# Seven block products instead of eight in the second layer's projection of a retention and feed-forward kernel

## The chip, the cores and the metric

One core of a Trainium2 chip runs the whole program. TensorE (PE) multiplies matrices, VectorE (DVE) and ScalarE (ACT) work on tiles element by element, GpSimd (POOL) does a little in the first stage, and SyncE (SP) issues nearly all transfers between DRAM and the chip's SBUF; products land in PSUM, eight banks of 128 x 512 floats, from which DVE and ACT read. The metric is the device time of one execution in microseconds, less is better.

## The reference, cut to what matters

```python
# q, k, v: (4, 8, 576, 64); seq 576, 8 heads
scores = matmul(q, k.T) / sqrt(64)
ret = scores * where(rel >= 0, gamma[h] ** rel, 0)      # rel = i - j
x = matmul(ret, v)                     # laid out as 2304 tokens x 512
# layer 1: w_gate, w_val (512 x 1536), w_out (1536 x 512)
g = x @ w_gate;  y = (g * sigmoid(g) * (x @ w_val)) @ w_out
# layer 2: w_in (512 x 2048), w_out (2048 x 512)
r = maximum(y @ w_in, 0);  out = (r * r) @ w_out        # 2304 x 512, float32
```

The weights arrive as 64-bit floating-point words (the inputs to the program are float64 for the weights) and have to be turned into float32 on the chip.

## The kernel before

**Three passes.** Each float32 operand is split into a high half that TensorE multiplies at one column a cycle (type fp32r) and a low half, the difference. `three` multiplies hi x hi, hi x lo and lo x hi into one PSUM bank, so each product of a 128 x 128 weight block with a slice of tokens is three matmuls. ACT makes the high half (`act.copy`), DVE the low half (a subtraction).

**Stages.** First the retention, 16 pairs of head pair and batch; its result is the tile `xy`, 4 slices of 128 features x 2304 tokens. Then layer 1 and layer 2, both over five chunks of tokens, four of 512 columns and chunk 2 of 256 (`CHUNKS`). In each chunk they go over the hidden blocks f of 128 (12 in layer 1, 16 in layer 2): the projection (`project`: 4 slices x 3 matmuls into bank `g` or `v`; layer 1 has two of these), the hidden values on ACT and DVE (`hidden1`: sigmoid and two products; `hidden2`: relu and square), their halves (`halves`, tiles `h_hi`, `h_lo`), and the output product of the hidden block before (`out1`, `out2`) into four banks `a0` to `a3` that add up over all f. Layer 1's output goes back into `xy`; layer 2's goes out to DRAM at the end of each chunk.

**Order.** In the layers the framework's scheduler sets the order on each engine: it lays the code's instructions out on a timeline of its own, so that rows can stand earlier or later than in the code. Layer 1 takes chunk 1 first, then the second half of chunk 0 (its first half was done during the retention and lies in DRAM as `part`), then 2, 3, 4. At a chunk's last hidden block the four slices of the next chunk's tokens are split (`split_x`, tiles `xh`, `xl`).

**Weights.** `prefetch` loads a unit (one weight block of 128 x 512, 512 KB of 64-bit words) on SP's queue into a `raw` tile or into a part of `xy` that lies idle; `conversion` is a generator that turns one unit into float32 `w` with three DVE operations on words, an addition (shown as ISA) and two ACT casts, and then into halves. `pump` advances it by one step between the other work: 4 steps a place in layer 1, 1 in layer 2. Layer 2's 32 units are converted in layer 1's last chunk and in layer 2's first chunk. Weights of layer 2 stay in SBUF as halves.

Of the kernel before, what the change touches and what calls it, by code (L numbers as in the profile page):

```python
# [9 lines left out]
F32 = mybir.dt.float32  # L10
# [17 lines left out]
CHUNKS = {  # L28
    1: [(0, 512), (512, 512), (1024, 256), (1280, 512), (1792, 512)],
    2: [(0, 512), (512, 512), (1280, 512), (1792, 512), (1024, 256)],  # L30
}
NCH = len(CHUNKS[1])
G0 = S // 2
# [12 lines left out]
PUMPS = {0: 1, 1: 4, 2: 1}  # L46
# [9 lines left out]
def retention_moe_kernel(  # L56
# [19 lines left out]
    raw_p = pool(ctx, "raw_p", 2)  # L76
    cv_p = pool(ctx, "cv_p", 1)
    xs_p = pool(ctx, "xs_p", 4)
    h_p = pool(ctx, "h_p", 2)
    t_p = pool(ctx, "t_p", 2)  # L80
    wa_p = pool(ctx, "wa_p", WA)
# [37 lines left out]
    order += [(2, what, f) for f in range(F2) for what in "io"]  # L119
# [4 lines left out]
    def prefetch(upto):  # L124

        while loads["next"] <= min(upto, len(order) - 1):
            i = loads["next"]
            if loads["pool"] < 2:
                loads["pool"] += 1
                raw_flat[i] = raw_p.tile([P, 1024], U32, tag="raw", name="raw")  # L130
                raw, back = raw_flat[i].rearrange("p (a n) -> p a n", a=2), None
            elif spare:
                back = spare.pop(0)
                raw = back.bitcast(U32)
            else:
                return
            loads["next"] += 1
            ph, what, f = order[i]
            src = (w1, w2)[ph - 1][f, :, ("gvo", "io")[ph - 1].index(what), :].bitcast(U32)
            sp.dma_start(out=raw, in_=src.rearrange("p (a n) -> p a n", a=2))  # L140
            raw_t[i] = raw, back
# [3 lines left out]
    homes = [in_a[u] for u in order[:3 * F1]] + [in_a[1, what, f] for f in range(F1) for what in "gvo"]  # L145
    homes = iter(homes)

    def weight_tiles(early=None):
        wp = wa_p if early or next(homes) else wb_p
# [10 lines left out]

    def conversion():
        ts = dve.tensor_scalar
        for i in range(len(order)):
            prefetch(max(i, min(i + 3, loads["cap"])))
            raw, back = raw_t[i]
            words = raw.rearrange("p a (n two) -> p a n two", two=2)
            low, high = words[:, :, :, 0], words[:, :, :, 1]
            low16 = raw.bitcast(U16).rearrange("p a (n four) -> p a n four", four=4)[:, :, :, 1]
            wt = cv_p.tile([P, 512], U32, tag="w", name="w", bufs=2)
            w_t[i] = wt  # L170
            w = wt.rearrange("p (a n) -> p a n", a=2)
            wf = w.bitcast(F32)
            act.activation(out=low, in_=low16, func=AF.Copy, scale=2.0**-13)
            act.activation(out=wf, in_=high.bitcast(F32), func=AF.Abs)
            yield
            ts(out=wf, in0=wf, scalar1=TINY, scalar2=HUGE, op0=ALU.max, op1=ALU.min)
            yield
            if i:
                parts_unit(i - 1)
            ts(out=w, in0=w, scalar1=3, scalar2=0x3FFFFFFF, op0=ALU.logical_shift_left, op1=ALU.bitwise_and)  # L180
            yield
            dve.scalar_tensor_tensor(
                out=w, in0=high, scalar=0xC0000000, in1=w, op0=ALU.bitwise_and, op1=ALU.bitwise_or
            )
            yield
            if back is None:
                adds = [(wt, raw_flat.pop(i).rearrange("p (n two) -> p n two", two=2)[:, :, 0])]
            else:
                adds = [(w[:, a], low[:, a]) for a in range(2)]
            for to, lo in adds:  # L190
                dve.tensor_tensor(out=to, in0=to, in1=lo, op=ALU.add)
# [7 lines left out]
        yield  # L199

    pumped = {"n": 0, "limit": 0}
    convert = conversion()

# [21 lines left out]
    xs, xs_w = {}, []  # L225

    def split_x(ph, n, cc):
        t0, m = CHUNKS[ph][n]
        src = xy[:, cc, t0:t0 + m]
        if ph == 2 and n == 0:  # L230
            xs_w.append(weight_tiles())
        if ph == 2 and n % 2 == 0:
            hi, lo = cut(xs_w[cc], 0, m)
        else:
            hi = xs_p.tile([P, N], F32R, tag="xh", name="xh")[:, :m]
            lo = xs_p.tile([P, N], F32R, tag="xl", name="xl")[:, :m]
# [13 lines left out]
    def project(ph, n, f, *cols, then=None):  # L250
# [3 lines left out]
        last = f == (F1, F2)[ph - 1] - 1  # L254
# [5 lines left out]
        if then is not None:  # L260
            for cc in range(CC):
                split_x(1, then, cc)
        elif 3 <= f < 3 + CC and (ph, n) != (2, NCH - 1) and (ph == 2 or n == NCH - 1):
            split_x(2, (n + 1) % NCH, f - 3)
# [41 lines left out]
    def hidden2(n, f):  # L306
        (ps,) = project(2, n, f, ("i", ("g", "v")[f % 2]))
        yield
        t = t_p.tile([P, 512], F32, tag="t", name="t")[:, :CHUNKS[2][n][1]]
        act.activation(out=t, in_=ps, func=AF.Relu)  # L310
        yield
        dve.scalar_tensor_tensor(
            out=t, in0=ps, scalar=0.0, in1=t, op0=ALU.max, op1=ALU.mult
        )
        yield
        halves((2, n, f), t)

    acc = {}
# [4 lines left out]
    def out1(n, f):  # L323

        f0, f1 = ((f // HALF) * HALF, (f // HALF + 1) * HALF - 1) if n == 0 else (0, F1 - 1)
# [10 lines left out]
        if n:  # L336
            assert all(back is None for _, back in raw_t.values())
# [14 lines left out]

    def out2(n, f):
        if f == 0:
            acc[2, n] = accs(CHUNKS[2][n][1] // P)
        h = hs.pop((2, n, f))
        ensure((2, "o", f))
        w = units[2, "o", f]
        for tt in range(CHUNKS[2][n][1] // P):
            three(acc[2, n][tt], cut(h, tt * P, P), w, f == 0, f == F2 - 1)  # L360
        if f == F2 - 1:
            for tt, a in enumerate(acc.pop((2, n))):
                if tt % 2 == 0:
                    o = raw_p.tile([P, 1024], U32, tag="raw", name="o_sb").bitcast(F32)
                t = o[:, (tt % 2) * 512:][:, :512]
                if tt % 2:
                    dve.tensor_copy(t, a)
                else:
                    act.copy(t, a)
                r0 = CHUNKS[2][n][0] + tt * P  # L370
                sp.dma_start(out=out[r0:r0 + P, :], in_=t)

# [190 lines left out]
    wb_p = pool(ctx, "wb_p", 3 * F1 - WA)  # L563
# [3 lines left out]

    segments = [(1, 1, 0, F1), (1, 0, HALF, F1)] + [(1, n, 0, F1) for n in range(2, NCH)]
    steps = [(ph, n, f, f == b - 1) for ph, n, a, b in segments for f in range(a, b)]
    follows = {s[1]: t[1] for s, t in zip(segments, segments[1:])}  # L570
    steps += [(2, n, f, False) for n in range(NCH) for f in range(F2)]

    def allowed(ph, n, f):
        if ph == 1 and n < NCH - 1:
            return 3 * F1
        return 3 * F1 + max(0, min(2 * (f - 1), 3 * (f - 1) - CC)) if ph == 1 else len(order)

    todo = [(1, 0, f) for f in range(HALF)]
    for ph, n, f, end in steps:
        pumped["limit"] = 5 * allowed(ph, n, f) + 7  # L580
        if f == 1 and (ph, n) in ((1, 1), (1, NCH - 1), (2, 0)):
            t0, m = CHUNKS[ph][n]
            loads["open"] = True
            loads["cap"] = (3 * F1 if n == 1 else len(order)) - 1
            spare.extend(xy[:, c:c + 2, t0:t0 + m] for c in (0, 2))
        if f == (F1, F2)[ph - 1] - 4:
            loads["open"] = False
            spare.clear()
        if (ph, n, f) == (1, 0, HALF + 1):
            sp.dma_start(out=xy[:, :, CHUNKS[1][0][0]:][:, :, :CHUNKS[1][0][1]], in_=part)  # L590
        step = hidden1(n, f, follows.get(n) if end else None) if ph == 1 else hidden2(n, f)
        for _ in step:
            pump(PUMPS[ph])
        for x in todo:
            (out1 if x[0] == 1 else out2)(*x[1:])
            if len(todo) > 1:
                pump(PUMPS[1])
        todo = [(ph, n, f)]
    out2(*todo[0][1:])
# [61 lines left out]
```

## Time and profile before

| what | value |
|---|---|
| time, median of 3 runs | 934.52 us (933.61 to 934.84) |
| span of the profiled execution | 934.4 us |
| PE busy, matmuls | 921.1 us (99%), 5146 |
| weight loads of PE (beside the matmuls) | 768.8 us (82%) |
| DVE busy | 465.9 us (50%), 850 instructions |
| ACT busy | 339.5 us (36%), 628 instructions |
| moved by DMA | 63.01 MB, 67 GB/s on average |

The profile is that of one execution; its span is the time from the first instruction to the last, and nothing lies around it that the table of runs would add (934.4 beside 934.52). Busy times are sums over all stages, so 50% for DVE is an average of stages in which it is nearly full and stages in which it is nearly idle. All instructions carry line 106, the helper through which the kernel records every operation, so groups are told apart by the names of tiles.

### The profile page before, as it was taken

The page shows a single profiled execution, that of the slowest core. Times are in us where ns is not written, and L with a number is a line of the kernel's source. Part 1 is how long each engine was busy: PE and PEld are TensorE (multiplying, and loading weights), DVE is VectorE, ACT ScalarE, POOL GpSimd, SP SyncE. Part 2 cuts the span into 40 slices and gives each one's busy share as a digit, 9 for nine tenths or more (in the row PEclk, how much of TensorE's full clock was granted, in tenths as well). Part 3 has the DMA queues.
Part 4 walks back from the last instruction along what each step waited for, and adds up shares of the span by engine and source line. Part 5 has one row for each costly group of instructions (what it writes and reads, how often), then busy time and mean ns, then how long its engine had stood idle before and what let it go on. Part 6 is the DMA issues. An engine that isn't in the chain of part 4 may idle for free.

```text
span 934.4 us, 12527 instructions
## 1 busy us (share of the span) xinstructions
PE 921.1 (99%) x5146; PEld 768.8 (82%) x5146; DVE 465.9 (50%) x850; ACT 339.5 (36%) x628; POOL 20.6 (2%) x39
## 2 busy tenths in 40 slices
PE   8899999999999999999999999999999999999998
PEld 6677788788889998888888888888888888888896
DVE  4678778797424242224898886242224223322332
ACT  3555455464212131113565564232223223222222
POOL 2111100000000000000000000000000000000000
PEclk9899999999999999999999999999999999999999
DMA  9767344442100000001334230010001000100000
GB/s 328 254 226 247 113 136 121 150 135 90 46 1 1 1 1 1 0 1 46 110 117 150 99 113 1 1 45 1 1 1 46 0 1 1 46 1 0 19 28 22
DMA packets 22168, 63.01 MB, mean 67 GB/s; under 512 B 2272, under 2 KB 3808, under 8 KB 22112
## 3 DMA queue, kind: packets, MB, share of 16 engines
q1 hardware_dynamic: 22112, 62.22, 19.7%
q8 instruction: 40, 0.66, 0.3%
q14 instruction: 16, 0.13, 0.1%
HBM read 56.44 MB, written 5.77 MB: 67 GB/s over the span
## 4 chain that ended last, share of the span: by engine, by line
PE 87%; DMA 6%; DVE 4%; ACT 2%; issue 1%; SPq 0%; ACTq 0%
PE a L106 33%; PE g L106 24%; PE v L106 24%; PE o L106 3%; PE s L106 2%; DMA raw<-in_w 2%; DVE w L106 2%; DMA xy<-in_w 2%; DMA kv_sb<-in_kv 1%; PE kvs L106 1%; DVE t L106 1%; DMA part<-part_sb 0%; DVE w_lo L106 0%; SPq L106 0%; ACT w L106 0%
## 5 line engine op out<-in xcount | busy, mean ns | idle before, releaser
L106 ACT ACTIVATE t<-g 128x512 f32<-128x512 f32 (+1 forms) x100 | 55.4, 554 | 208.5 <-PE g L106 208.3
L106 ACT CAST h_hi<-t 128x512 fp32r<-128x512 f32 (+1 forms) x134 | 77.1, 576 | 118.6 <-DVE t L106 112.9
L106 DVE TENSOR_TENSOR h_lo<-t,h_hi 128x512 fp32r<-128x512 f32 (+1 forms) x134 | 85.2, 636 | 68.6 <-ACT h_hi L106 68.1
L106 PE MATMUL g<-xh,w_hi 128*128 128x512 f32 (+1 forms) x304 | 113.9, 375 | 0.0
L106 PE MATMUL v<-xh,w_hi 128*128 128x512 f32 (+1 forms) x304 | 113.8, 375 | 0.0
L106 PE MATMUL g<-xl,w_hi 128*128 128x512 f32 (+1 forms) x304 | 113.3, 373 | 0.1
L106 PE MATMUL g<-xh,w_lo 128*128 128x512 f32 (+1 forms) x304 | 113.3, 373 | 0.0
L106 PE MATMUL v<-xh,w_lo 128*128 128x512 f32 (+1 forms) x304 | 113.2, 373 | 0.0
L106 PE MATMUL v<-xl,w_hi 128*128 128x512 f32 (+1 forms) x304 | 113.2, 372 | 0.0
L106 PE MATMUL a<-w_lo,h_hi 128*128 128x512 f32 x288 | 112.3, 390 | 0.0
L106 PE MATMUL a<-w_hi,h_hi 128*128 128x512 f32 x288 | 112.2, 390 | 0.0
L106 PE MATMUL a<-w_hi,h_lo 128*128 128x512 f32 x288 | 109.8, 389 | 0.0
L106 DVE TENSOR_TENSOR t<-g,t 128x512 f32<-128x512 f32 (+1 forms) x60 | 38.2, 636 | 85.8 <-ACT t L106 85.5
L106 PE MATMUL a<-h_lo,w_hi 128*128 128x512 f32 (+1 forms) x216 | 79.3, 367 | 0.4 <-DVE h_lo L106 0.4
L106 PE MATMUL a<-h_hi,w_lo 128*128 128x512 f32 (+1 forms) x216 | 78.6, 366 | 0.0
L106 DVE SCALAR_TENSOR_TENSOR t<-g,t 128x512 f32<-128x512 f32 (+1 forms) x40 | 25.5, 638 | 105.2 <-ACT t L106 105.1
L106 PE MATMUL a<-h_hi,w_hi 128*128 128x512 f32 (+1 forms) x216 | 76.8, 366 | 0.7 <-ACT h_hi L106 0.7
L106 DVE SCALAR_TENSOR_TENSOR t<-v,t 128x512 f32<-128x512 f32 (+1 forms) x40 | 25.6, 639 | 92.3 <-ACT t L106 92.0
L106 DVE TENSOR_SCALAR w<-w 128x512 f32<-128x512 f32 (+1 forms) x136 | 57.3, 422 | 23.1 <-ACT w L106 21.8
L106 PEld LDWEIGHTS g<-xh,w_hi 128*128 128x128 f32 x304 | 57.3, 188 | 10.4 <-ACT raw L106 0.2
L106 PEld LDWEIGHTS g<-xl,w_hi 128*128 128x128 f32 x304 | 57.3, 188 | 10.3 <-DVE xl L106 0.5
L106 PEld LDWEIGHTS v<-xh,w_hi 128*128 128x128 f32 x304 | 57.3, 188 | 10.2
(82 smaller groups left out, 1474.2 us busy)
## 6 DMA issues: line engine op xcount, KB each, us to landing
raw<-in_w SPq DMA_DIRECT2D x51, 512.0 KB, 3.6
xy<-in_w SPq DMA_DIRECT2D x17, 512.0 KB, 3.7
qk_sb<-in_qk SPq DMA_DIRECT2D x15, 576.0 KB, 4.9
kv_sb<-in_kv SPq DMA_DIRECT2D x15, 576.0 KB, 3.9
out<-o_sb SPq DMA_DIRECT2D x18, 256.0 KB, 2.2
part<-part_sb SPq DMA_DIRECT2D x4, 256.0 KB, 2.8
xy<-part SPq DMA_DIRECT2D x1, 1024.0 KB, 5.2
mask_sb<-in_mask SPq DMA_DIRECT2D x4, 128.0 KB, 7.2
```

What stands on the lines that cost most here:

```text
L106: i = op(*args, **kw)
```

## The change

Layer 1's hidden blocks and products stay. Three things change.

**Seven products.** Layer 2's tokens are taken as 3 pairs of blocks of 384 columns (`M2`; block p and the block 1152 tokens behind it), its input features as two halves of 256, its hidden blocks as 8 pairs. For each pair of tokens and each pair of hidden blocks, a *system* n of 24, the four output blocks (2 hidden blocks x 2 token blocks) come from seven products of a combined weight block with a combined token block instead of eight plain ones. Each product is 2 slices x 3 passes = 6 matmuls of 384 columns. Products 1, 6, 7 and 4 add up in one bank (`g`) and are read off between (`x`), 5 and 3 in `v` (`y`), and 2 in `a0` (`z`); DVE adds the parts, squares and splits. The output product (`out_tile`) now takes 128 tokens and four hidden blocks at a time in banks `a1` to `a3` and adds to `xy`, which collects the sum over four groups and is stored at the last.

**Weight operands.** `conversion2` turns layer 2's words into float32 during layer 1 and stores them in DRAM (`wst`). The seven combined and split weight operands of a pair of hidden blocks (`stationary`, 11 DVE operations and 7 casts) are made in layer 1 for the first two pairs (`STAGED`) and in the first systems of layer 2 for the other six (`build`), and stored in DRAM (`win`). The systems of the later token pairs load them (`product`: 256 KB each), and output weights are loaded as float32 and split again for each group (`load_out`).

**Layer 1's order.** Chunks 1, 0, 3, 4 and then 2, the 256-wide one, last; there the hidden blocks 6 to 9 come first so that their weights' room (`freed`) can take the combined token blocks (`renew`, `operand`). Conversion is pumped at a pace (`PACE`, `SLOW`) per step. In chunk 2's end `stationary` operands of the tokens for the first pair are made.

```diff
-    2: [(0, 512), (512, 512), (1280, 512), (1792, 512), (1024, 256)],
+M2 = 384
+PAIRS2 = NT // (2 * M2)
+FP = F2 // 2
+PACE = {0: 1, 3: 1.5, 4: 1.5, 2: 0.8}
+SLOW = 1.25
+STAGED = 2
+FREED = range(6, 10)
+PORD = (1, 0, 2)
...
+    def stationary(k, w0, w1_, s1, to):
+        tt = dve.tensor_tensor
+        a11, a12, a21, a22 = (w[:, a:a + 256] for w in (w0, w1_) for a in (0, 256))
+        to(1, a11)
+        tt(out=s1, in0=a21, in1=a22, op=ALU.add)
+        to(2, a12)
+        to(5, s1)
+        tt(out=a21, in0=a11, in1=a21, op=ALU.subtract)
+        tt(out=a11, in0=s1, in1=a11, op=ALU.subtract)
+        to(6, a11)
+        to(7, a21)
+        tt(out=a12, in0=a12, in1=a11, op=ALU.subtract)
+        to(4, a22)
+        to(3, a12)
...
+            if j >= 2 * STAGED:
+                give_back(j)
+                late_store = wst[what, f], wf
+                continue
...
+            def to(i, src):
+                if len(stores) > 1:
+                    sp.dma_start(out=stores[-2][0], in_=stores[-2][1].bitcast(F32))
+                at = stage[len(stores) % 4]
+                split(at[:, :256], at[:, 256:], src)
+                stores.append((win[j // 2][:, ROW[i]], at))
...
+    segments = [(1, every), (0, every[HALF:]), (3, every), (4, every)]
+    segments.append((2, list(FREED) + [f for f in every if f not in FREED]))
...
+    wi_p = pool(ctx, "wi_p", 3)
...
+    def build(k):
+        w0, w1_ = (in_p.tile([P, 512], F32, tag=f"in{x}", name="w_in") for x in range(2))
+        for x, w in enumerate((w0, w1_)):
+            sp.dma_start(out=w, in_=wst["i", 2 * k + x])
...
+        def to(i, src):
+            w = wi_p.tile([P, 512], F32R, tag=f"wi{i}", name="wi")
+            split(w[:, :256], w[:, 256:], src)
+            built[k, i] = w
+            later.append((win[k][:, ROW[i]], w.bitcast(F32)))
...
+    def product(n, i, dst, first, last):
+        w = built.pop((n, i), None)
+        if w is None:
+            w = wi_p.tile([P, 512], F32R, tag=f"wi{i}", name="wi")
+            sp.dma_start(out=w.bitcast(F32), in_=win[n % FP][:, ROW[i]])
+        for c in range(2):
+            hi, lo = w[:, c * P:(c + 1) * P], w[:, 256 + c * P:256 + (c + 1) * P]
+            xh, xl = (x[:, c] for x in xo[i])
+            for k, (a, b) in enumerate(((hi, xh), (hi, xl), (lo, xh))):
+                at = c * 3 + k
+                pe.matmul(dst, a, b, start=first and at == 0, stop=at == 5, skip_group_check=True)
...
+    def slot(n, i):
...
+        if i == 1:
+            act.copy(a[:, 0], x)
+        elif i == 2:
+            tt(out=a[:, 0], in0=s["z"], in1=a[:, 0], op=ALU.add)
+            dve.scalar_tensor_tensor(out=a[:, 0], in0=a[:, 0], in1=a[:, 0], **relu2)
+        elif i == 6:
+            act.copy(b[:, 0], x)
+        elif i == 7:
+            act.copy(b[:, 1], x)
+            tt(out=b[:, 1], in0=s["y"], in1=b[:, 1], op=ALU.add)
+        elif i == 4:
+            act.activation(out=a[:, 1], in_=x, func=AF.Relu)
+            dve.scalar_tensor_tensor(out=a[:, 1], in0=x, in1=a[:, 1], **relu2)
+            hidden(n, "a", a)
+        elif i == 3:
+            tt(out=b[:, 0], in0=s["y"], in1=b[:, 0], op=ALU.add)
+            dve.scalar_tensor_tensor(out=b, in0=b, in1=b, **relu2)
+            hidden(n, "b", b)
...
+    def load_out(g):
+        for f in range(4 * (g % 4), 4 * (g % 4) + 4):
+            w = wo_p.tile([P, 2, 512], F32R, tag="wo", name="wo")
+            sp.dma_start(out=w[:, 1].bitcast(F32), in_=wst["o", f])
+            act.copy(w[:, 0], f32(w[:, 1]))
+            tt(out=w[:, 1], in0=f32(w[:, 1]), in1=f32(w[:, 0]), op=ALU.subtract)
...
+    def out_tile(g, which, j):
...
+        for k in range(4):
...
+            three(acc_, (hi, lo), (w[:, 0], w[:, 1]), k == 0, k == 3)
...
+        if q == 0:
+            act.copy(home, src)
+        else:
+            tt(out=home, in0=src, in1=home, op=ALU.add)
+        if q == 3:
+            sp.dma_start(out=out[t0:t0 + P, :].rearrange("p (c q) -> p c q", c=CC), in_=home)
...
+    for n in range(last + 2):
...
+        if n and n % 2 == 0:
+            load_out(n // 2 - 1)
+        for x in ((1, n), (7, n - 1), "o", (2, n), (4, n - 1), "o", (6, n), (3, n - 1), "o", (5, n)):
```

**Where the instructions stand.** At the end of layer 1's chunk 1, before the four splits of the next chunk's tokens, DVE has these rows before (`w` a weight unit, `t` and `h_lo` the hidden values and their low half, `xl` the low half of a slice of tokens; numbers tell tiles apart):

```order
L106 ISA w_2150<-raw_2148,w_2150 128x1024
L106 TENSOR_TENSOR t_2381<-g_2355,t_2381 128x512
L106 TENSOR_TENSOR t_2381<-v_2356,t_2381 128x512
L106 TENSOR_TENSOR h_lo_2386<-t_2381,h_hi_2385 128x512
L106 TENSOR_TENSOR xl_2428<-xy_81,xh_2427 128x512
L106 TENSOR_TENSOR xl_2432<-xy_81,xh_2431 128x512
L106 TENSOR_TENSOR xl_2436<-xy_81,xh_2435 128x512
L106 TENSOR_TENSOR t_2443<-g_2401,t_2443 128x512
L106 TENSOR_TENSOR xl_2440<-xy_81,xh_2439 128x512
L106 TENSOR_TENSOR t_2443<-v_2402,t_2443 128x512
L106 TENSOR_TENSOR h_lo_2448<-t_2443,h_hi_2447 128x512
```

And after, at the same place (`raw` now also holds the low halves of the staged operands, `s1` the sum that two of them share):

```order
L116 TENSOR_TENSOR t_2409<-g_2383,t_2409 128x512
L116 TENSOR_TENSOR s1_2728<-w_2675 128x256
L116 TENSOR_TENSOR w_2675<-w_2622,w_2675 128x256
L116 TENSOR_TENSOR raw_2620<-s1_2728,raw_2620 128x256
L116 TENSOR_TENSOR w_2622<-s1_2728,w_2622 128x256
L116 TENSOR_TENSOR t_2409<-v_2384,t_2409 128x512
L116 TENSOR_TENSOR raw_2618<-w_2675,raw_2618 128x256 x2
L116 TENSOR_TENSOR w_2622<-w_2622 128x256
L116 TENSOR_TENSOR raw_2620<-w_2622,raw_2620 128x256
L116 TENSOR_TENSOR h_lo_2414<-t_2409,h_hi_2413 128x512
L116 TENSOR_TENSOR raw_2620<-w_2622,raw_2620 128x256
L116 TENSOR_TENSOR xl_2456<-xy_81,xh_2455 128x512
```

The operations of the combined operands stand between the two products and the low half of the last hidden block but one, and ahead of the splits `xl`.

On SP, before, the only rows from layer 1's last chunk on are loads of `in_w2` into `raw` and `xy` and the stores of the output. After, these rows stand at the switch to layer 2 (`wi` weight operands of a product, `win` their place in DRAM, one for each pair of hidden blocks, `wst` float32 weights, `wo` output weights, `w_in` the weights that `build` combines):

```order
L116 DMA wi_4990<-win_83 128x512
L116 DMA w_in_4999<-wst_98 128x512
L116 DMA w_in_5000<-wst_100 128x512
L116 DMA wi_5003<-win_82 128x512
L116 DMA wi_5043<-win_82 128x512
L116 DMA wo_5103<-wst_91 128x512
L116 DMA wo_5107<-wst_93 128x512
L116 DMA wo_5111<-wst_95 128x512
L116 DMA wi_5023<-win_83 128x512
L116 DMA wo_5115<-wst_97 128x512
L116 DMA w_in_5129<-wst_102 128x512
L116 DMA win_84<-wi_5014 128x512
```

Loads for the first two systems (`win_82`, `win_83`), for `build` (`w_in`) and for the output product (`wo`) share one queue, and the first stores of built operands (`win_84`) stand right behind them.

On PE, before, a block of layer 2 is twelve matmuls of the projection into `g` or `v` and twelve of the output product of the block before into `a0` to `a3`; here two projections follow each other, and then the output product begins:

```order
L106 MATMUL v_5931<-xh_5028,w_hi_5386 128x512
L106 MATMUL v_5931<-xl_5029,w_hi_5386 128x512
L106 MATMUL v_5931<-xh_5028,w_lo_5387 128x512
L106 MATMUL g_5963<-w_hi_4088,w_hi_4092 128x512
L106 MATMUL g_5963<-w_lo_4089,w_hi_4092 128x512
L106 MATMUL g_5963<-w_hi_4088,w_lo_4093 128x512
L106 MATMUL g_5963<-w_hi_4168,w_hi_4092 128x512
L106 MATMUL g_5963<-w_lo_4169,w_hi_4092 128x512
L106 MATMUL a0_5491<-w_hi_5375,h_hi_5915 128x512
L106 MATMUL a0_5491<-w_lo_5376,h_hi_5915 128x512
L106 MATMUL a1_5492<-w_hi_5375,h_hi_5915 128x512
```

After, in the middle of layer 2 (`z` is product 2 of one system, `g_7040` product 4 of the system before it, `oacc` an output tile; `xo` token operands, `ho` the hidden halves):

```order
L116 MATMUL z_7212<-xo_lo_6937,wi_7213 128x384
L116 MATMUL z_7212<-xo_hi_6936,wi_7213 128x384 x2
L116 MATMUL z_7212<-xo_lo_6937,wi_7213 128x384
L116 MATMUL z_7212<-xo_hi_6936,wi_7213 128x384
L116 MATMUL oacc_7237<-wo_7024,ho_hi_6950 128x512 x2
L116 MATMUL oacc_7237<-wo_7024,ho_lo_6951 128x512
L116 MATMUL oacc_7237<-wo_7028,ho_hi_6950 128x512
L116 MATMUL g_7040<-xo_hi_7107,wi_7223 128x384
L116 MATMUL g_7040<-xo_lo_7108,wi_7223 128x384
L116 MATMUL g_7040<-xo_hi_7107,wi_7223 128x384 x2
L116 MATMUL g_7040<-xo_lo_7108,wi_7223 128x384
```

The order of the code has product 4 right behind product 2 and an output tile behind it; in PE's order four matmuls of that output tile stand ahead of product 4. At the end of chunk 2 PE's rows likewise have the next hidden block's projection ahead of the output product of the block before.

## Rows read from the trace of the kernel before

**Rows 1.** the page's busy times, and three of its rows of 40 slices

```profile
PE 921.1 (99%) x5146; PEld 768.8 (82%) x5146; DVE 465.9 (50%) x850; ACT 339.5 (36%) x628; POOL 20.6 (2%) x39
...
DVE  4678778797424242224898886242224223322332
...
PEclk9899999999999999999999999999999999999999
DMA  9767344442100000001334230010001000100000
```

**Rows 2.** what PE waited for: us in total, times, longest

```profile
PE a L106 <- ACT h_hi L106: 0.7, 1, 0.7
PE a L106 <- DVE h_lo L106: 0.4, 2, 0.3
```

**Rows 3.** the chain that ended last: start, us, what, matmuls

```profile
212.00 2.72 PE g L106 x12
...
292.77 1.44 PE v L106 x12
```

**Rows 4.** stretches: length, busy us (count) of PE, PEld, DVE, ACT, POOL, clock, DMA

```profile
300.00:340.00 40.00, 40.00 (x330) 39.78 (x329) 13.75 (x31) 9.39 (x22) 0.00 (x0) 1.00 0.00 1
...
540.00:900.00 360.00, 360.00 (x1626) 299.56 (x1625) 126.09 (x205) 106.76 (x183) 0.00 (x0) 1.00 0.05 18
```

**Rows 5.** timeline of DVE: start, us, operation, count

```profile
283.65 0.41 DVE L106 TENSOR_TENSOR xl<-xy,xh 128x256 fp32r<-128x256 f32 x1
283.98 0.68 DVE L106 TENSOR_TENSOR t<-v,t 128x512 f32<-128x512 f32 x1
...
290.26 1.88 DVE L106 TENSOR_TENSOR xy<-a,xy 128x512 f32<-128x512 f32 x3
```

**Rows 6.** end of chunk 1: timelines of ACT and DVE, and the chain

```profile
231.98 0.67 ACT L106 ACTIVATE raw<-raw 128x512 uint32<-128x512 uint16 x1 [1.67 <-DMA raw<-in_w]
232.54 0.60 ACT L106 CAST h_hi<-t 128x512 fp32r<-128x512 f32 x1
233.05 1.66 ACT L106 CAST xh<-xy 128x512 fp32r<-128x512 f32 x3
...
233.18 0.69 DVE L106 TENSOR_TENSOR h_lo<-t,h_hi 128x512 fp32r<-128x512 f32 x1 [3.72 <-ACT h_hi L106]
...
233.75 3.00 PE a L106 x12
242.19 2.72 PE a L106 x12
```

**Rows 7.** DMA issues: count, KB each, median us to landing

```profile
raw<-in_w SPq DMA_DIRECT2D x51, 512.0 KB, 3.6
...
out<-o_sb SPq DMA_DIRECT2D x18, 256.0 KB, 2.2
part<-part_sb SPq DMA_DIRECT2D x4, 256.0 KB, 2.8
```

**Rows 8.** stretches of the first stage, columns as in rows 4

```profile
0.00:20.00 20.00, 16.83 (x176) 12.92 (x178) 7.58 (x17) 5.95 (x13) 4.22 (x13) 1.00 0.88 313
...
28.00:30.00 2.00, 0.38 (x12) 0.27 (x6) 1.44 (x5) 0.85 (x3) 0.00 (x0) 1.00 0.82 283
30.00:32.00 2.00, 2.00 (x28) 1.64 (x27) 1.92 (x5) 1.55 (x5) 1.57 (x2) 0.80 0.73 245
32.00:34.00 2.00, 2.00 (x22) 1.67 (x20) 1.85 (x3) 0.60 (x2) 0.00 (x0) 0.50 1.00 400
34.00:36.00 2.00, 1.77 (x30) 1.37 (x26) 0.00 (x0) 1.06 (x3) 0.00 (x0) 0.85 1.02 354
```

**Rows 9.** the last rows of the timeline

```profile
929.87 0.69 DVE L106 COPY o_sb<-a 128x512 f32<-128x512 f32 x1 [1.30 <-PE a L106]
930.25 0.81 SPq L106 DMA_DIRECT2D out<-o_sb  x2
```

More of the change, by code (lines that the diff above doesn't have):

```diff
@@ L165, in conversion @@
             raw, back = raw_t[i]
[L166 to L191, printed above, removed]
+            for n, wt in enumerate(words(raw, back, raw_flat.pop(i, None))):
+                w_t[i] = wt
+                if n == 2:
+                    if i:
+                        parts_unit(i - 1)
+                else:
+                    yield
             del raw_t[i]
@@ new lines, in conversion2 @@
+    def conversion2():
+        pair, late_store = [], None
+        for j, (what, f) in enumerate(seq2):
+            load2(j + 3)
+            for n, wt in enumerate(words(*raw2[j])):
+                if n == 3 and late_store is not None:
+                    sp.dma_start(out=late_store[0], in_=late_store[1])
+                if n != 2:
+                    yield
+            wf = wt.bitcast(F32)
+            if j >= 2 * STAGED:
+                give_back(j)
+                late_store = wst[what, f], wf
+                continue
+            pair.append((raw2[j][0].bitcast(F32R), wf))
+            if j % 2 == 0:
+                continue
+            stage, stores = [raw[:, x] for raw, _ in pair for x in range(2)], []
+            def to(i, src):
[4 more added lines that the diff above has]
+                stores.append((win[j // 2][:, ROW[i]], at))
+            s1 = cv_p.tile([P, 256], F32, tag="s1", name="s1")
+            yield from stationary(j // 2, pair[0][1], pair[1][1], s1, to)
+            for dst, at in stores[-2:]:
+                sp.dma_start(out=dst, in_=at.bitcast(F32))
+            yield
+            give_back(j - 1)
+            give_back(j)
+            pair = []
+        sp.dma_start(out=late_store[0], in_=late_store[1])
+        yield
@@ L201, in retention_moe_kernel, with pump2 @@
     pumped = {"n": 0, "limit": 0}
     convert = conversion()
+    convert2 = conversion2()
+    def pump2(k=1):
+        for _ in range(k):
+            next(convert2, None)
     def pump(k=1):
@@ L304, in hidden1_early @@
             halves((1, 0, f), early_t.pop(f), early=True)
[L306 to L318, printed above, removed]
+    acc, ends = {}, {}
     def accs(n_acc):
@@ L578, in retention_moe_kernel @@
[L578 to L586, printed above, removed]
+    every = list(range(F1))
+    segments = [(1, every), (0, every[HALF:]), (3, every), (4, every)]
@@ new lines, in retention_moe_kernel, with halves_of, operand @@
+    segments.append((2, list(FREED) + [f for f in every if f not in FREED]))
+    steps = [(n, f, at, at == len(fs) - 1) for n, fs in segments for at, f in enumerate(fs)]
+    follows = {s[0]: t[0] for s, t in zip(segments, segments[1:])}
+    ends.update({n: (fs[0], fs[-1]) for n, fs in segments})
+    tt = dve.tensor_tensor
+    def halves_of(p):
+        ta = p * M2
+        return [xy[:, c:c + 2, t:t + M2] for c in (0, 2) for t in (ta, NT // 2 + ta)]
+    xo = {}
+    def operand(i, src):
+        hi = xo_p.tile([P, 2, M2], F32R, tag=f"xh{i}", name="xo_hi")
+        lo = xo_p.tile([P, 2, M2], F32R, tag=f"xl{i}", name="xo_lo")
+        act.copy(hi, src)
+        tt(out=lo, in0=src, in1=f32(hi), op=ALU.subtract)
+        xo[i] = hi, lo
@@ L587, in retention_moe_kernel @@
+    pace = {"due": 0.0}
+    todo = [(0, f) for f in range(HALF)]
+    for n, f, at, end in steps:
+        t0, m = CHUNKS[1][n]
+        if at == 1 and n in (1, 3, 4):
+            loads["open"], loads["cap"] = True, 3 * F1 - 1
+            (spare if n == 1 else free2).extend(xy[:, c:c + 2, t0:t0 + m] for c in (0, 2))
+        if at == F1 - 4 - (n > 2):
             loads["open"] = False
             spare.clear()
-        if (ph, n, f) == (1, 0, HALF + 1):
+            free2[:] = [x for x in free2 if x is None]
+        if (n, at) == (0, 1):
@@ L594, in retention_moe_kernel @@
+        if at == 0 and n:
+            assert all(back is None for _, back, _ in raw2.values())
         for x in todo:
-            (out1 if x[0] == 1 else out2)(*x[1:])
+            out1(*x)
             if len(todo) > 1:
                 pump(PUMPS[1])
-        todo = [(ph, n, f)]
-    out2(*todo[0][1:])
+        todo = [(n, f)]
+        if n == 2 and at == len(FREED):
+            freed.close()
+            xo_p = pool(ctx, "xo_p", 1, side="right")
+        if n == 2 and at > len(FREED):
+            renew(PORD[0], (1, 2, 5, 6, 7, 4, 3)[at - len(FREED) - 1])
@@ new lines, in retention_moe_kernel, with hidden @@
+    hid = {}
+    def hidden(n, which, c):
+        hi = ho_p.tile([P, 2, M2], F32R, tag=f"h{which}", name="ho_hi")
+        lo = ho_p.tile([P, 2, M2], F32R, tag=f"l{which}", name="ho_lo")
+        act.copy(hi, c)
+        tt(out=lo, in0=c, in1=f32(hi), op=ALU.subtract)
+        hid[n, which] = hi, lo
+    wos = {}
+    def load_out(g):
[4 more added lines that the diff above has]
+            tt(out=w[:, 1], in0=f32(w[:, 1]), in1=f32(w[:, 0]), op=ALU.subtract)
+            wos[g, f % 4] = w
@@ new lines, in retention_moe_kernel @@
+    last = PAIRS2 * FP - 1
+    make = iter(())
+    for n in range(last + 2):
+        for _ in make:
+            pass
+        if STAGED <= n + 1 < FP:
+            make = build(n + 1)
+        tiles = []
+        if n >= 3:
+            g, which = divmod(n - 3, 2)
+            tiles = [(g, "ab"[which], j) for j in range(3)]
+        if n and n % 2 == 0:
+            load_out(n // 2 - 1)
+        for x in ((1, n), (7, n - 1), "o", (2, n), (4, n - 1), "o", (6, n), (3, n - 1), "o", (5, n)):
+            if x == "o":
+                if tiles:
+                    out_tile(*tiles.pop(0))
+                continue
+            i, k = x
+            if not 0 <= k <= last:
+                continue
+            slot(k, i)
+            next(make, None)
+            next(make, None)
+            if k % FP == FP - 1 and k < last and i != 6:
+                for i in (5, 6) if i == 5 else (i,):
+                    renew(PORD[k // FP + 1], i)
@@ L603 @@
+    g = 4 * PAIRS2 - 1
+    for which in "ab":
+        for j in range(3):
+            out_tile(g, which, j)
 _OUT = ((NT, DM), "float32")
```

205 lines of the change are left out of this document (144 added, 61 removed).

## Prediction

> **What bounds the kernel now.** I read the page's first two parts first: TensorE (PE) is busy for 921.1 of 934.4 us, VectorE (DVE) for half of that, and the granted clock is full after the first fortieths [rows 1]. A busy PE may still be a PE that waits inside its busy time, so the waits come next: from the feed-forward layers they name only 0.7 and 0.4 us, both on halves of a hidden tile [rows 2]. Then the chain that ended last: in the layers it is PE row after PE row, twelve matmuls at a time, 2.72 us for twelve of 512 columns and 1.44 us for twelve of 256 [rows 3]. So the layers run at PE's pitch, 226.7 ns and 120.0 ns a matmul. The 256 columns between them cost 106.7 ns, 0.417 ns each, which is the 2.4 GHz level; the rest, 13.3 ns, comes with each matmul whatever its width. In the stretches of 256-wide matmuls and of layer 2 the clock is 1.00, and DVE is busy for 35% of layer 2 [rows 4]. What the change takes from PE in layer 2 comes off the end, unless a new wait eats it.
>
> **What is removed.** Layer 2's projection to the hidden layer is 16 blocks x 4 slices x 3 passes = 192 matmuls a chunk: 768 of 512 columns and 192 of 256, 768 x 0.2267 + 192 x 0.1200 = 197.1 us. Afterwards there are 24 systems (3 pairs of token blocks x 8 pairs of hidden blocks), each of 7 products of 6 matmuls: 1008 of 384 columns. No row has that width; by the line through the two that are there a matmul costs 0.160 + 0.0133 = 0.1733 us, in all 174.7 us. **The gain is 22.4 us.** The line could be wrong only between two measured points: if the fixed part grew from 13.3 to 20 ns, 6.8 us would be lost. The 864 matmuls of the second output projection and all of layer 1 keep their widths; layer 1 only takes its 256-wide chunk last.
> The Trainium skill ("TensorE: Matmul & The Clock Gate", Back-to-back issue gap) gives N/2.4 + 2.5 ns for one warm matmul. By that the projections go from 186.7 to 163.8 us, a gain of 22.9 us; the rows show some 11 ns more per matmul, at both widths, and the sum above goes by them.
>
> **What is added to DVE and ACT.** Three 512-wide DVE operations follow each other in 1.88 us where one lasts 0.69, a pitch of 0.60; a 256-wide one has 0.33 (283.65 to 283.98) [rows 5]. That makes 0.47 at 384 and 0.87 at 768. A system of layer 2 needs five of 384 and three of 768 (4.9 us), two and a quarter output additions (1.35) and two splits of output weights (1.2): 7.5 us. PE needs 42 x 0.1733 + 36 x 0.2267 = 15.4 us for it. Systems 2 to 7 also have their weight operands built, 11 x 0.33 = 3.6 us more: 11.1 of 15.4. On average DVE is covered; without output tiles (the first systems) PE needs only 7.3 us a system, and the cover is gone. The seven operands of the next pair cost 9.6 us of DVE, spread over two systems of 30.9 us: hidden.
>
> **First switch: the end of chunk 1.** The operands of the first two pairs of hidden blocks are made here. In the kernel before ACT sits behind loads until 231.98, the hidden half follows at 232.54, and twelve output matmuls take 3.00 instead of 2.72 us; the next twelve of that kind start at 242.19 [rows 6]. In the new order DVE has 11 more operations of 256 here and ACT seven casts; stores (2.8 us to landing, the nearest row) and the next load (3.6) stand in the chain [rows 7]. From 226.6 on I counted along both engines: the hidden half comes at 232.4 (no later than before), but the last slice of x is behind store, load and two conversions: store issued at 232, landed 234.7, load landed 238.4, the slice ready at 240.6, wanted at 239.6. One us of wait for the one that was there, then little slack for one more step. I take +0.5; bounds -1.1 (the old wait goes and none comes) and +4 (two landings 1.5 us later each).
>
> **Conversion in chunks 3, 4 and 2.** One and a half weights a step of 8.2 us is some 3.3 us of DVE beside 1.9 of its own work. The hidden chain has 36 matmuls (8.2 us) of slack. Nothing, covered by PE; uncovered it would be what DVE has in the stretch from chunk 4 on now, which PE did not notice either [rows 1, 2]. At the end of chunk 2 seven casts of 768 stand together, but PE's rows have the next projection moved ahead there, and by the same count no matmul waits.
>
> **Layer switch.** T is the end of layer 1's last product. Five product loads stand before the first SP row that waits for it, two of them released 4.1 and 3.4 us ahead of T (34 and 28 matmuls of 0.12). All others follow T, in one queue, stores of built operands among them, each of which waits for DVE. 313 GB/s at a share of 0.88 is 356 at full share [rows 8]: 0.74 us for 256 KB, and some 2 us of landing. The seventh product's load is the seventh behind T, there at T + 7.0, wanted at T + 6.2: **0.8 us**. The tenth product (first of system 2) uses the PSUM bank of system 0 and waits until DVE has read it. DVE's queue holds 22 operations before that, 10 us from T + 2.4: T + 12.3, where PE is ready at T + 10.4: **some 2 us**. Together 3 us; bounds 0 (the next products ordered in between would cover it) and 10 (B below).
> A pause has a second price. At 28 to 30 us PE was busy for 0.38 of 2 us; in the three stretches behind it the clock was 0.80, 0.50 and 0.85 [rows 8], so (0.20 + 0.50 + 0.15) x 2 = 1.7 us of full speed were lost. I add **1.7**; bounds 0 and 3.4 (twice).
>
> **Tail.** The last copy starts at 929.87, its store is issued by 931.1, the span ends at 934.4 [rows 9]. Afterwards there is one addition of the same width and a store in four times as many pieces: +0.3; bounds 0 and 2.2, one more landing [rows 7].
>
> **Sum.** 934.4 - 22.4 + 0.5 + 3.0 + 1.7 + 0.3 = 917.5. The median of the runs stands 0.1 above the profiled span: **917.6 us**, 1.8% faster.
>
> **Rivals.**
> A, the forecast: PE stays the bound, the losses are those above: 912.5 to 923. Chance 0.67.
> B, layer 2's first eight systems are bound by their loads. Sixty transfers of 256 KB stand between T and the last weight that the build of system 7 needs. At 0.74 us they are through at T + 46, where PE wants it at T + 56. At 245 GB/s, the rate of the stretch 30 to 32 [rows 8], each takes 1.07 us: T + 66, 10 us late, with two more pauses of the clock 13: 931. For it: SP takes them in order, and every store waits for DVE. Against: in that stretch the engines were not full. 923 to 932, chance 0.19.
> C, the other side: the hidden path of layer 2. Products 1, 6, 7 and 4 of a system add up in one bank, and ACT must have read it after each. Between 7 and 4 stand an output tile and product 2, 3.8 us. If product 4 had to wait 0.7 us more in each of 24 systems, 16.9 us, the net gain would be gone: the read would have to come 4.5 us after product 7, behind five casts of 768 (some 0.8 each). For it: PE's order has product 4 three matmuls into the next output tile, not right behind product 2, so that the plan itself has ACT late there. Against: ACT has 5 us of work in 15.4. At 1.5 us a system the time is 917.6 + 36 = 954. Chance 0.09, a third of it within 0.2% of before.
> D, the new matmuls lose the full clock. At half of it one costs 0.333 us: 161 us more, 1079 us. The 256-wide stretch ran at 1.00 [rows 4]. Chance 0.02. [...]
> E, the gain is larger than all losses but the losses are almost nothing: 911 to 912.5. Chance 0.03.
>
> **How the numbers follow.** 0.2% (1.9 us) is about what a measurement here can tell from no change. Faster: A, B (all but its edge) and E, 0.88; same: a third of C, 0.03; slower: the rest of C and D with B's edge, 0.09. The range 911.5 to 929 leaves out the edge of B and all of C and D, some 0.17.
>
> **What would show it.** Right: 1008 matmuls of 384 columns at a pitch of 0.173 us; layer 2, about 393 us from its first to its last matmul now (768 + 864 matmuls of 512 columns, 192 of 256), at about 371 plus the losses; PE's waits concentrated in the 20 us behind the last output matmul of layer 1, on DVE and on loads, with a clock below 1 right behind; DVE at about half in the later systems. Wrong: a pitch other than 0.173; waits on ACT or DVE that repeat in every system (C); waits on loads of built or stored operands over the first 60 us of layer 2 (B); new waits in chunks 3 and 4, where I have none.

## The result and the profile after

The changed kernel takes 926.0 us (median of 4 runs, 925.32 to 928.99) against 934.5: ratio 0.9916, 95% interval 0.9901 to 0.9931. The gain is 8.5 us by the medians and 7.8 by the ratio, half of the 16.9 forecast or a little less; 926.0 lies inside the stated range, but the losses are more than twice the 5.5 us that I had in the sum.

The page of after, the lines that answer to [rows 1]:

```profile
PE 905.3 (98%) x5194; PEld 777.3 (84%) x5194; DVE 585.0 (63%) x1043; ACT 369.1 (40%) x694; POOL 20.6 (2%) x39
...
DVE  4787778799626763377534669858754567554553
...
PEclk9999999999999999999999999999999999999999
DMA  9767244443512461144400079745574555564102
```

PE is still the bound, with 15.8 us less. What it waited for from the layers on (us in total, times, longest; compare [rows 2]):

```profile
PE z L116 <- DMA wi<-win: 2.2, 1, 2.2
PE g L116 <- ACT xh L116: 1.3, 1, 1.3
PE a L116 <- ACT h_hi L116: 0.9, 2, 0.5
PE a L116 <- DVE h_lo L116: 0.2, 1, 0.2
```

That is 4.6 us in all, and no wait repeats. So most of the missing gain is no wait. It shows in the chain (start, us, what, matmuls), first in layer 1's chunk 3:

```profile
352.41 2.81 PE g L116 x12
355.23 2.81 PE v L116 x12
358.04 2.80 PE a L116 x12
...
372.02 2.72 PE v L116 x12
374.74 2.81 PE a L116 x12
```

Twelve matmuls of 512 columns take 2.72 us, as in [rows 3], or 2.81: 234 ns a matmul instead of 226.7, at the same full clock. The slow ones are those of hidden blocks 6 to 9, in every chunk. In layer 2 of after:

```profile
703.58 2.12 PE g L116 x12
705.70 2.75 PE oacc L116 x12
```

2.12 / 12 is 176.7 ns for 384 columns, where the line through the two known widths gave 173.3; output tiles take 229, not 226.7.

The account, from the starts of all matmuls in both traces (a start-to-start time above the nominal 226.7, 173.3 or 120.0 ns counts as pitch, from 20 ns on as a stop):

| term | forecast, us | measured, us |
|---|---|---|
| projections of layer 2 (seven products) | -22.4 | -19.1 |
| layer 2's output tiles | 0 | +1.9 |
| layer 1, 512 columns +4.4, 256 columns -0.4 | 0 | +4.0 |
| stops in layer 1 | +0.5 | +1.6 |
| layer switch with the clock | +4.7 | +4.0 |
| tail | +0.3 | +0.3 |
| retention stage | 0 | -2.8 |
| sum, span 934.4 to 924.3 | -16.9 | -10.1 |

The retention stage is no part of the change: its clock dips [rows 8] differ from execution to execution, and the profiled one of before had a large one (clock 0.73 from 30 to 40 us, where after has 1.00). In every run below the time stands 1.8 us above the span, so that execution took some 936.2 us, 1.7 above its median. That the span (934.4) and the median (934.52) of before stand side by side is chance, and not a sign that nothing lies around the span. 10.1 less 1.7 is 8.4, beside the 8.5 of the medians. For the same reason totals of single kernels scatter by 2 to 7 us with the mean clock (0.988 to 1.000), and the sums by pitch and stops decide below.

### The profile page after: what moved, and what is told of

It reads as the page before. It is cut to its first block, busy times and chain, and to the rows that moved or that the text cites. A ratio compares the mean times of both kernels' runs of the same rounds, so it can differ in the third digit from the quotient of the medians.

```text
span 924.3 us, 13507 instructions
## 1 busy us (share of the span) xinstructions
PE 905.3 (98%) x5194; PEld 777.3 (84%) x5194; DVE 585.0 (63%) x1043; ACT 369.1 (40%) x694; POOL 20.6 (2%) x39
## 4 chain that ended last, share of the span: by engine, by line
PE 75%; DMA 12%; DVE 7%; ACT 4%; issue 2%; SPq 1%; ACTq 0%; DVEq 0%
PE oacc L116 21%; PE g L116 21%; PE v L116 16%; PE a L116 9%; DMA raw<-in_w 7%; DVE w L116 3%; PE o L116 3%; PE s L116 2%; PE z L116 2%; DMA kv_sb<-in_kv 2%; ACT raw L116 1%; DMA xy<-in_w 1%; ACT w L116 1%; PE kvs L116 1%; DVE t L116 1%
## 5 line engine op out<-in xcount | busy, mean ns | idle before, releaser
L116 PE MATMUL oacc<-wo,ho_hi 128*128 128x512 f32 x576 | 181.2, 392 | 0.0
L116 PEld LDWEIGHTS oacc<-wo,ho_hi 128*128 128x128 f32 x576 | 107.5, 188 | 17.7
L116 PE MATMUL oacc<-wo,ho_lo 128*128 128x512 f32 x288 | 111.7, 390 | 0.0
L116 PE MATMUL g<-xo_hi,wi 128*128 128x384 f32 x384 | 111.1, 340 | 0.1
L116 PEld LDWEIGHTS g<-xo_hi,wi 128*128 128x128 f32 x384 | 71.4, 189 | 2.3 <-DVE ca L116 0.4
L116 ACT ACTIVATE raw<-raw 128x512 uint32<-128x512 uint16 x52 | 35.1, 674 | 85.0 <-DMA raw<-in_w 83.1
L116 PE MATMUL g<-xo_lo,wi 128*128 128x384 f32 x192 | 65.4, 340 | 0.0
L116 PEld LDWEIGHTS oacc<-wo,ho_lo 128*128 128x128 f32 x288 | 54.1, 188 | 11.1
L116 DVE TENSOR_TENSOR xy<-oacc,xy 128x512 f32<-128x512 f32 x54 | 37.1, 687 | 34.5 <-PE oacc L116 34.3
L116 PE MATMUL v<-xo_hi,wi 128*128 128x384 f32 x192 | 57.5, 339 | 0.0
```

What stands on the lines that cost most here:

```text
L116: i = op(*args, **kw)
```

## The experiments

The edits are shown shortened.

**Where operands start.** In the compiled program nearly all tiles that the layers' matmuls read start at 128 modulo 512 bytes of their partition. The pools that the change takes from the right end of SBUF (`wr_p`: weights of blocks 6 to 9; later `xo_p`: layer 2's token operands) start at 480. Theory 1 was that such a start slows a matmul; theory 2 that other engines and transfers get in its way. Three runs put an unused tile ahead of these pools, one shifts the kernel before as a whole.

```diff
+    pool(ctx, "pad", 1, side="right").tile([P, 88], F32)   # 352 bytes
     wb["wr"] = pool(freed, "wr_p", 3 * len(FREED), side="right")
```

> The changed kernel with 352 unused bytes ahead of the two pools on the right side of SBUF, so that the weights of layer 1's hidden blocks 6 to 9 and layer 2's token operands start at 128 instead of 480 modulo 512, like all other tiles. Theory 1 (a matmul is slowed by an operand whose rows start 32 bytes off a multiple of 64): the 512-wide matmuls of blocks 6 to 9 go from 234 to 226.7 ns, the 384-wide ones from 176.7 to 173.3, the output tiles from 229.4 to 226.7; 4.4 us in layer 1 and 5.1 in layer 2 come back, 916.5 us. Theory 2 (other engines or transfers compete for SBUF in these stretches): no pitch changes, 926.0 us.

> The same padding for the weights of blocks 6 to 9 alone. Theory 1: only layer 1's 4.4 us come back, 921.6 us, and 256-wide matmuls of these blocks go back from 117 to 120 ns (0.4 us lost), so 922.0; layer 2's pitches stay at 176.7 and 229.4 ns. Theory 2: 926.0 us.

> The same padding for the token operands of layer 2 alone. Theory 1: the 384-wide pitch goes to 173.3 ns (3.3 us); if the slow output tiles are a follow-up of these products, they go to 226.7 too (1.8 us more): 920.9 us; if they have a cause of their own, 922.7. Layer 1 keeps 234 ns in blocks 6 to 9. Theory 2: 926.0 us.

> The kernel before with one unused tile of 32 bytes at the start of SBUF, so that every operand starts at 160 instead of 128 modulo 512. Theory 1: 3228 matmuls of 512 columns each 7.6 ns longer, 624 of 256 some 2.8 ns shorter: 934.5 + 24.5 - 1.7 = 957 us; up to 968 if the moving operand adds its own 3.4 ns. Theory 2: nothing changes, 934.5 us.

Measured: pad_layer1 923.6 us, pad_both 924.9, pad_layer2 925.8, before_shift32 934.5 (ratio to before 1.0000, 0.9985 to 1.0014). The chain of pad_layer1 over the same blocks of chunk 3:

```profile
351.86 2.72 PE g L116 x12
354.58 2.72 PE v L116 x12
357.30 2.72 PE a L116 x12
```

With the pad layer 1's pitch loss falls from 4.7 to 0.3 us, what it was before the change. Theory 2 falls: engines and transfers are the same there. But theory 1 in its form falls too, since a kernel whose operands all start 32 bytes further on is not slower. And in layer 2 the pad brings only 0.8 of 5.6 us: the products lose 1.4 us less (3.3 to 1.9), but the output tiles, whose own operands did not move, lose 0.7 more (2.3 to 2.9). That second part none of the runs explains.

**Distance, not place.** Two runs give the four blocks other starts, and one moves only the weights of the kernel before.

```diff
-    wb["wr"] = pool(freed, "wr_p", 3 * len(FREED), side="right")
+    for f, n in zip((6, 7, 8, 9), (8, 48, 16, 8)):   # offsets_b: 64, 32, 8, 16
+        pool(freed, f"pad{f}", 1, side="right").tile([P, n], F32)
+        wb[f"wr{f}"] = pool(freed, f"wr{f}_p", 3, side="right")
```

> The changed kernel with the weights of layer 1's hidden blocks 6, 7, 8 and 9 in pools of their own that start at 448, 256, 192 and 160 modulo 512 (480 in the change, 128 for all other operands). Theory 1a (the two operands of a matmul must start at the same place modulo 512): all four blocks at 234 ns. Theory 1b (the distance must be a multiple of 64): 448, 256 and 192 at 226.7, 160 at 234. Theory 1c (the place itself counts, 96 modulo 128 is slow): all four at 226.7.

> The same with 224, 96, 64 and 0 modulo 512 for blocks 6, 7, 8 and 9. Theory 1a: all four at 234 ns. Theory 1b: 224 and 96 at 234, 64 and 0 at 226.7. Theory 1c: the same as 1b here, so that 160 in the run before tells these two apart.

```diff
+    pool(ctx, "pad", 1).tile([P, 8], F32)   # 32 bytes, kernel before
     wa_p = pool(ctx, "wa_p", WA)
```

> The kernel before with 32 unused bytes ahead of its weight pools alone: weights start at 160 modulo 512, the tiles of x and of the hidden halves stay at 128. Theory 1a (a matmul of 512 columns takes 233 to 234 ns where its two operands start at different places modulo 512, whichever is the stationary one): all of layer 1 but the output products whose hidden halves lie in weight tiles (72), layer 2's output products and its projections in the chunks whose x lies in xs tiles are slow, some 2800 matmuls by 6.7 ns: 934.5 + 18.7, less some 1.2 us at 256 columns: 952 us. Where both lie in weight tiles (projections of layer 2's chunks 0 and 2) 226.7 ns. If only the weight as the stationary operand counts, layer 2's output products (weights moving) stay at 226.7: 946.

Both runs of the other starts are single ones. Chain of offsets_a (projections of blocks 7 and 9, at 256 and 160), of offsets_b (7 and 8, at 96 and 64), and of before_offset32 (layer 1, then layer 2):

```profile
342.50 2.79 PE g L116 x12
345.29 2.80 PE v L116 x12
...
359.27 2.79 PE g L116 x12
362.06 2.80 PE v L116 x12
```

```profile
344.71 2.80 PE g L116 x12
347.51 2.79 PE v L116 x12
...
353.11 2.76 PE g L116 x12
355.87 2.75 PE v L116 x12
```

```profile
397.61 2.80 PE v L107 x12
400.41 2.80 PE a L107 x12
...
564.13 2.79 PE a L107 x12
...
568.05 1.59 PE g L107 x7
```

All nine other starts that were tried are slow; 64 is the mildest (230 ns). before_offset32 takes 950.2 us (ratio 1.0171, 1.0147 to 1.0196): 32 unused bytes cost 15 us. Layer 2's projections in chunk 0, where x lies in weight tiles too, stay at 227 ns (1.59 / 7), and its output products, whose moving operand is the weight, are slow. So it is theory 1a: what counts is that the stationary and the moving operand start at the same place modulo 512, whichever lies where. A distance of 256 bytes is not among those tried, so a period of 256 would fit these runs as well. At 256 columns the same mismatch makes a matmul shorter at most starts (113 to 118 ns, not 120; no change at 256 and 0). Why, these runs don't say.
The Trainium skill ("SBUF — State Buffer", SBUF: two separate sides) says that among the engines only the port pair that GpSimd and VectorE share causes contention, and that PE never waits on anyone. That is said of waits between engines and not of PE's own two operands, and the measured 226.7 and 234 ns, with nothing changed but 352 unused bytes, are an effect that it doesn't name.

**Changes of width.** Once all operands agree, a long stretch of one width runs at 226.7 or 173.3 ns exactly, and only the first six matmuls of 384 and the first nine of 512 behind a change of width are slower. Chain of pad_both (a stretch with a change ahead of it, and 12 and 6 of 384 columns):

```profile
707.08 1.06 PE z L116 x6
...
713.03 1.04 PE v L116 x6
714.07 2.76 PE oacc L116 x12
716.84 1.06 PE v L116 x6
717.90 2.08 PE g L116 x12
```

The products behind others (1.04, 2.08) have 173.3 ns; those behind an output tile have 1.06, and the tile itself 2.76 instead of 2.72. One run changes width less often, one lets the kernel before change it more often.

```diff
-for x in ((1, n), (7, n-1), "o", (2, n), (4, n-1), "o", (6, n), (3, n-1), "o", (5, n)):
+for x in ((1, n), (7, n-1), "o", (2, n), (4, n-1), (6, n), (3, n-1), "o", "o", (5, n)):
```

> The kernel with both pads, and in each system the second output tile moved behind product 3, so that layer 2 changes between matmuls of 384 and of 512 columns 114 times instead of 178. Theory 5 (what is left of the slow pitch in layer 2 is paid after each change of width, 4.8 us over 178 changes, 27 ns each): the loss falls to 3.1 us, 923.1 if no wait is added. Theory 6 (it belongs to the output tiles or to the start of a product): it stays at 4.8 us, 924.9. If PE now waits for ACT or DVE it shows as stops in every system (rival C of the prediction).

```diff
-    2: [(0, 512), (512, 512), (1280, 512), (1792, 512), (1024, 256)],
+    2: [(0, 512), (512, 384), (896, 384), (1280, 384), (1664, 384), (2048, 256)],
```

> The kernel before with layer 2's tokens cut into one chunk of 512, four of 384 and one of 256: no seven products, all operands at 128 modulo 512. PE's sum by pitch is 2.5 us more than before. Theory 5 (each change between widths costs 27 to 30 ns): four chunks x 32 changes are 3.8 us more, in the first six to nine matmuls behind each change; 940.8 us. Theory 6 (the loss belongs to the seven products or the output tiles of the change): 937.0, and 173.3 and 226.7 ns throughout.

Measured: fewer_switches 923.2 us (ratio 0.9886, 0.9863 to 0.9908), layer 2's pitch loss 3.4 us for 114 changes, against 4.8 for 178: 30 and 27 ns a change. Its chain has the tiles in pairs, 24 matmuls in 5.48 us, and 24 nominal ones are 5.44: the 40 ns come once, not for each tile:

```profile
707.31 5.48 PE oacc L116 x24
```

before_384 took 941.7 us in its one run; its pitch loss is 4.2 us above before for 128 changes, 33 ns each, without any of the seven products. Theory 6 falls. The kernel before had the same thing in its last chunk, where 256 columns alternate with 512; its chain, in rows that I had not looked at for this:

```profile
879.49 2.75 PE a L106 x12
...
883.91 2.75 PE a L106 x12
```

**The layer switch.** The stretch of after that answers to [rows 8] (length, busy of PE, PEld, DVE, ACT, POOL, clock, DMA share, GB/s):

```profile
540.00:560.00 20.00, 17.72 (x87) 16.60 (x86) 15.66 (x35) 10.91 (x26) 0.00 (x0) 0.91 1.02 368
```

PE stopped for 2.3 us at product 2 of system 1, whose load was late, ran the next ten matmuls in 320 ns each, the lower clock level (1.5 us), and stopped for 0.3 us more behind DVE. Two runs try to take the stops away.

```diff
-            sp.dma_start(out=w[:, 1].bitcast(F32), in_=wst["o", f])
+            with ExitStack() as behind:
+                if g == 0:   # behind the load of product 5 of system 1, on SP
+                    behind.enter_context(tc.issue_after(loaded[1, 5]))
+                sp.dma_start(out=w[:, 1].bitcast(F32), in_=wst["o", f])
```

> The kernel with both pads, and the first four loads of output weights issued on SP behind the product loads of system 1. Theory 3 (at the layer switch product 2 of system 1 waits because its load stands behind three output weights, 3 x 0.74 us): the stop of 2.3 us before that product falls to under 0.8 and the eleven matmuls at half clock behind it go, 3 to 4 us less than with both pads (924.9), about 921.5. Theory 4 (the transfers as a whole are too many for these 20 us): another load is late by as much, the sum of stops stays at about 4 us, 924.9.

```diff
-STAGED = 2
+STAGED = 3
```

> The kernel of fewer_switches with the operands of three pairs instead of two made in layer 1. Theory 3' (the stops at the layer switch, 4 us, come from what stands in DVE's and SP's queues there: 3.6 us of DVE and 0.5 MB less for system 2): stops fall to some 1.5 us, 2.5 us less than fewer_switches, which had 919.6 at clock 1.00 and 921.2 at 0.997. Theory 4 (the product loads of systems 1 and 2 are late because the transfers are full): the stops stay at 4 us. In layer 1 the 11 DVE operations and 7 casts more may add a wait of up to 1 us.

wo_later: 925.0 us. PE stops at the same product as before, for a shorter time. What PE waited for, with both pads and then in wo_later:

```profile
PE g L116 <- ACT xh L116: 2.2, 1, 2.2
PE z L116 <- DVE wo L116: 2.2, 1, 2.2
```

```profile
PE z L116 <- DVE wi L116: 1.4, 1, 1.4
PE g L116 <- DVE ca L116: 0.8, 1, 0.8
```

The view names DVE for `z`, but it is still the load: the weights of system 1 are loaded, not built, and a view can only infer who ended a wait for several semaphores. By the semaphore events the last part of this load lands at 547.38 us in after, 546.87 with both pads and 545.73 in wo_later, and in each the matmul starts 0.14 us behind that; the first of the `wi` operations of DVE that the view names for wo_later ends at 545.88, when the matmul has started (545.87). Counted from layer 2's first matmul the load lands after 8.5 us in after and with both pads, and after 7.6 in wo_later: the three output weights are gone from ahead of it, but two loads of `w_in` stand there instead. So theory 3 was right that the place of the load counts, and wrong that it would be in time: the stop before `z` falls from 2.4 to 1.5 us, the later stops, behind DVE, stay at some 1.6, and all stops of layer 2 sum up to 3.3 us, against 4.0 with both pads. That is nearer to theory 4.

staged3: the stops of layer 2 fall from 4.1 us in fewer_switches to 2.2, as theory 3' had it in direction, but layer 1 has 8.6 us of stops in place of 4.9. Of these 3.7 us some 2.3 are at the end of chunk 1, where PE's wait for `xh` is 2.4 us and some ten matmuls at the lower clock level follow (427 ns each). That is not shown to be a price of the third pair: the kernel with both pads, where two pairs are made in layer 1, has the same there (2.2 us above, and the lower clock behind it). The stops of 1.7 us at 447 to 457 us stand in staged3 alone. At 921.7 us (ratio 0.9865, 0.9850 to 0.9880) it is the fastest of these kernels, by less over fewer_switches than these two scatter.

**Rival C.** One run tries to give the hidden path the short distance that C was about.

```diff
-for x in (..., "o", (2, n), (4, n-1), (6, n), (3, n-1), "o", "o", (5, n)):
+for x in (..., (2, n), (4, n-1), (6, n), (3, n-1), "o", "o", "o", (5, n)):
```

> The kernel with both pads, and the three output tiles of a system behind each other after product 3. Between product 7 and product 4, which add up in one bank, stands only product 2 (1.04 us) where there was an output tile as well (3.8 us). Rival C of the prediction: ACT must have read the bank, PE waits 0.5 to 1.5 us in each of 24 systems, 12 to 36 us more, 936 to 960. If the scheduler's order or ACT's pace covers it: no stops, 923 us like fewer_switches.

924.0 us, stops only at the layer switch (3.8 us), none in the later systems. PE's rows still have most of an output tile between products 7 (in the first `g`) and 4 (in the second), because the scheduler lays it there. Its chain:

```profile
701.56 2.08 PE g L116 x12
703.64 1.04 PE z L116 x6
704.68 2.54 PE oacc L116 x11
707.22 2.10 PE g L116 x12
```

So the short distance itself was not tried, and C is refuted only for orders that this scheduler makes.

## Why the prediction was off

- **What bounds the kernel, and the form of the sum:** right. PE stays the bound; no new wait repeats; 1008 matmuls of 384 columns take the place of 768 of 512 and 192 of 256. Layer 2 takes 380.6 us from its first to its last matmul: about the 371 of the forecast, plus 4.4 of stops and 5.6 of pitch. DVE is fuller in the later systems than the half that I had, 51 to 65% from 600 to 900 us.
- **The gain, 22.4 us:** the step that failed. It took one matmul's time from its width alone ("the line could be wrong only between two measured points"). The line holds: 173.3 ns is what a 384-wide matmul takes in a long stretch with operands in step. But 176.7 is what it takes in this kernel: 3.3 us less gain. 1.4 of them are the start of the token operands and go with the pad; 1.9 stand behind changes of width. The bound of 20 ns for the fixed part covered its size, not its cause.
- **"The 864 matmuls ... and all of layer 1 keep their widths":** they do, and not their times. The output tiles lose 1.9 us because they now alternate with another width, layer 1 loses 4.0 because four blocks' weights moved to a pool that starts at 480 modulo 512. I had read the moved pool as a matter of room only. These three sizes, 9.2 us, are more than the whole shortfall of 8.4; the rest of the account nearly cancels.
- **First switch, +0.5:** right in mechanism, short in size. The slice of x came behind store, load and two conversions, as counted: 1.46 us of wait instead of 1.0, with the load in 4.8 us, not 3.6. This trace is on the low side: in the ten traces of kernels with these rows the same stop is 1.2 to 2.6 us, 2.2 in the middle, and in three of them (pad_both, outs_together, staged3) the lower clock follows and costs 1.6 us more. The store left on the count (228.7, where 232 less the 2.8 us of the retention stage is 229.2). The chain of after there, from the store to the slice and the matmul that waits for it:

```profile
228.71 2.39 DMA win<-raw
...
231.16 4.76 DMA raw<-in_w
...
237.62 0.62 ACT xh L116
238.24 0.04 issue
238.28 0.50 PE g L116
```

- **"Conversion in chunks 3, 4 and 2. Nothing":** wrong by 1.1 us. At 348 us PE waits for a hidden half (`h_hi`) that stands behind a conversion on ACT, and the conversion waits for its load. The chain of after there:

```profile
342.91 4.60 DMA raw<-in_w
...
347.61 0.68 ACT raw L116
348.29 0.51 ACT h_hi L116
348.80 0.02 issue
348.82 0.70 DVE h_lo L116
```

- **Layer switch, 3.0 with 1.7 for the clock:** 2.6 and 1.5 by the starts of matmuls, 4.4 with the first matmul behind each stop (4.0 net of the stops that before had in layer 2). The total is near by luck, since the parts were shifted: the load cost 2.3 us where I had 0.8 (it landed 8.5 us behind T, where the count had 7.0), the bank 0.3 where I had 2.
- **Rivals:** B did not come: transfers fill the queue at 368 GB/s from 540 to 560, but only one load was late. C and D did not come either; but for the ten matmuls behind the stop at the switch the 384-wide stretches run at clock 1.00.
- **Tail, +0.3:** right. The time outside the span, taken as 0.1, is 1.8; the profiled execution of before was 1.7 slower than its median, and the two cancel.

## What to carry to other kernels

Before pricing a matmul, look where its two operands start: a pool taken from the other end of SBUF, or 32 bytes more ahead of one group of tiles, put the stationary and the moving operand out of step modulo 512 bytes and cost 3% of every 512-wide matmul so placed here. Count how often PE changes between widths (27 to 33 ns each) and keep like products together. And when a wait names an engine whose work was done long before, look for a transfer that landed just then. Read the pitch of each kind of matmul in each stretch of the trace, since such losses hide inside busy time and no list of waits names them.

## What the runs showed of the hardware that I had not expected

- 512 columns: 226.7 ns with operands in step modulo 512 bytes, 230 (start 64 against 128) to 234 out of step; 256 columns: 120 in step, 113 to 118 out of step for most starts.
- Behind a change of width the loss is spread over the first six matmuls of 384 columns and the first nine of 512, about 25 and 40 ns in all, and then it is gone. What makes it, and the dependence on the start, stays open.
